# Block sums of a Strassen-like GEMM: kept in DRAM for the second layer, shared with GpSimd in the first, block maxima sought earlier

## The chip, the core and the metric

The kernel runs on one core of one Trainium2 chip. The metric is the device time of one execution in microseconds (us). A core has TensorE (PE, matmuls), VectorE (DVE), ScalarE (ACT), GpSimd (POOL) and SyncE (SP); in this kernel SP issues nearly all DMAs, in one queue and in order.

## What is computed

Two layers, the same weights in both. Sequence 2048, width 1024, 32 heads of 32, hidden width F = 3584.

```python
def _A_ref(x, wqkv, wo):                      # sliding local attention, window 8, dilation 2
    qkv = x @ wqkv ...                        # q, k, v per head
    idx = pos[:, None] - arange(8) * 2        # 8 keys per query: every second position back
    o = softmax(q . k[idx] * Dh**-0.5, masked where idx < 0) @ v[idx]
    return o @ wo
def _B_ref(x, w1, b1, w2, b2):                # MLP over the tokens
    u = gelu(einsum("bsd,sf->bdf", layernorm(x), w1) + b1)
    return transpose(einsum("bdf,fs->bds", u, w2) + b2)

x = x + _A_ref(layernorm(x)); x = x + _B_ref(layernorm(x))      # layer one
x = x + _A_ref(layernorm(x)); x = x + _B_ref(layernorm(x))      # layer two
```

## The kernel before

Each layer runs in four stages: values and attention by unit (16 units, two visits each), the output projection `out_proj` (16 row tiles, each followed by its layer norm, which writes the tile `h2[c][i]`), the first token GEMM `gemm1`, and the second, `gemm2`. TensorE is fed in a written order (`in_order`); DVE, ACT, POOL and SP operations are chained by `chain_`, which makes each come after the one before it on its engine.

**gemm1** is the stage that the change touches. F is cut into 14 blocks of 256 columns. Block 0 is done plainly (`plain`, 64 matmuls). Blocks 1 to 13 use a seven-product scheme on 2 x 2 quarters: the tokens are split by dilation class c (0, 1), the width into two halves of 512, the block's columns into two halves of 128. In fp16 that needs

- token sums T0 to T3 once in a layer (`token_sums`, `token_sums2`): T0 = B12 - B11 and T2 = B22 - B12 on POOL, T1 = B22 - T0 on DVE, T3 = B21 - T1 on POOL, eight pieces of 128x512 each;
- for every block four weight sums S0 to S3 (`weight_sum`, tile `Sw`, 128x1024 each): S0 = a01 + a11, S1 = S0 - a00, S2 = a00 - a01, S3 = a10 - S1.

Before it can be summed in fp16, a block's bf16 weights are scaled by a power of two, so that they don't leave fp16's range. The power comes from the block's largest magnitude: `top` (two DVE reductions over 128x2048, line 627), `share` (a DMA of the 128 maxima to DRAM and a DMA that broadcasts them back, lines 631 and 633), `power` (five small DVE operations, lines 638 to 643, which write the factor `cs` and its inverse `ci`). `scale_w` (line 647, ACT, two operations of 128x2048) rewrites the weights; the Gelu takes `ci` as its scale. Layer one looks for all the powers; layer two reuses them, but scales and sums the weights again.

A block fb of the loop from line 715 on, as TensorE sees it; each product is eight matmuls of 128x512, and the names P1 to P7 are used below:

| product | what | waits for, or is followed by |
|---|---|---|
| P1 | a00 x B11 into `pa` | scaled weights; then ACT copies `pa` to X (line 670) |
| P2 | a11 x T3 of the **previous** block (`product4`) | then DVE adds it to Y of that block (`py<-py,m`), ACT Gelu |
| P3 | a10 x B21, added into `pa` | then ACT Gelu of `pa` (line 674) |
| P4 | S0 x T0 into `pd` | `pa` and `pd` are halves of one PSUM tile: P4 waits for the Gelu of `pa` |
| P5, P6 | S1 x T1, S2 x T2 | ACT copies `pd` to Z after P4; DVE adds P5 to X, P6 to Y |
| P7 | S3 x B22, added into `pd` | then DVE adds `pd` to X (`px<-px,s` or `px<-px,acc`) |

Z + Y is added on POOL (`pz<-pz,py`, 128x512 in fp32). The DVE order within a block of layer one, with `nxt` = fb + 1: add `pd` to X of the previous block; `power(nxt)`; first `top` of block fb + 2; add P2 to Y of the previous block; second `top`; then S2, S0 of `nxt`, add to X, S1, add to Y, S3. The ACT order: Gelu of Z and X of the previous block, copy to X, `scale_w(nxt, 0)`, Gelu of Y of the previous block, Gelu of `pa`, `scale_w(nxt, 1)`, copy to Z.

```python
in_order(product, pa, a(fb, 1, 0), B21, False)              # P3
chain_(A, gelu, fb, 0, 0, pa)
...
in_order(product, pd, Ss[fb][:, 0], Tk(0), True, False)     # P4
```

The tiles `Sw` rotate through two buffers, which in the attention hold the zero-padded queries `qB`; the weight tiles `w` rotate through nine buffers, in which the attention's weights lie before. In the attention most of the queries are copied into `qB` by SP DMAs (line 407).

Of the kernel before, what the change touches and what calls it, by code (L numbers as in the profile page):

```python
# [10 lines left out]
ALU = mybir.AluOpType  # L11
# [17 lines left out]
def kernel(  # L29
# [38 lines left out]
    SHIFT = 14.0  # L68
    assert D == H * DH and NT == 16 and NI == 8 and NG == 8 and HG == 4
# [96 lines left out]
    ci = const.tile([P, NFB], FP32, name="ci")  # L166
    kT = [pers.tile([P, SC], BF16, name=f"kT{n}") for n in range(2)]
# [13 lines left out]
    mxd = dram.tile([NFB, P, DIL], FP32, name="mxd")  # L181

# [420 lines left out]

    def gemm1(h2, g, first):
# [7 lines left out]
        def token_sums():  # L612
            for i in range(NI):
                chain_(G, tt, nc.gpsimd, T[:, 0, i, :], B12[i], B11[i], ALU.subtract)
            for i in range(NI):
                chain_(G, tt, nc.gpsimd, T[:, 2, i, :], B22[i], B12[i], ALU.subtract)

        def token_sums2():
            for i in range(NI):
                chain_(V, tt, nc.vector, T[:, 1, i, :], B22[i], T[:, 0, i, :], ALU.subtract)  # L620
            for i in range(NI):
                chain_(G, tt, nc.gpsimd, T[:, 3, i, :], B21[i], T[:, 1, i, :], ALU.subtract)
# [12 lines left out]
        def power(fb):  # L635
            m = st("m", [P, 1])
            e = st("e", [P, 1])
            nc.vector.tensor_reduce(out=m[:], in_=bc_[fb][:], op=ALU.max, axis=AX.X)
            nc.vector.tensor_scalar(out=m[:], in0=m[:], scalar1=2.0 ** -100, scalar2=None, op0=ALU.max)
            nc.vector.tensor_scalar(out=e[:].bitcast(INT32), in0=m[:].bitcast(INT32), scalar1=0x7F800000, scalar2=None,  # L640
                                    op0=ALU.bitwise_and)
            nc.vector.tensor_scalar(out=ci[:, fb:fb + 1], in0=e[:], scalar1=2.0 ** -13, scalar2=None, op0=ALU.mult)
            return nc.vector.reciprocal(out=cs[:, fb:fb + 1], in_=ci[:, fb:fb + 1])

# [4 lines left out]
        def a(fb, c, fl):  # L649
            return w1s[fb][c][:].bitcast(FP16)[:, :, fl * P:(fl + 1) * P]  # L650

        def weight_sum(fb, n):
            if n == 2:
                Ss[fb] = qp.tile([P, 4, NI, P], FP16, name="Sw", tag="q")
            q = [Ss[fb][:, k] for k in range(4)]
            i0, i1, op = [(a(fb, 0, 1), a(fb, 1, 1), ALU.add), (q[0], a(fb, 0, 0), ALU.subtract),
                          (a(fb, 0, 0), a(fb, 0, 1), ALU.subtract), (a(fb, 1, 0), q[1], ALU.subtract)][n]
            return tt(nc.vector, q[n], i0, i1, op)
# [13 lines left out]
        def gelu(fb, fl, dc, src):  # L672
            ft = fb * GF + fl
            return nc.scalar.activation(out=g[fb][:, fl, dc * 512:(dc + 1) * 512], in_=src, func=ACT.Gelu_apprx_tanh,  # L674
                                        bias=b1_sb[:, ft:ft + 1], scale=ci[:, fb:fb + 1])

        def prepare(fb):
            if fb >= NFB:
                return
            for c in range(DIL):  # L680
                chain_(A, scale_w, fb, c)

        def finish12(fb):
            chain_(V, tt, nc.vector, X[fb][:], X[fb][:], ad[fb][:, 1, :], ALU.add)
            chain_(A, gelu, fb, 0, 1, X[fb][:])
# [5 lines left out]
        def finish21(fb):  # L691
            chain_(V, tt, nc.vector, Y[fb][:], Y[fb][:], f_[fb][:], ALU.add)
            chain_(A, gelu, fb, 1, 0, Y[fb][:])

        token_sums()
        for c in range(DIL):
            if first:
                chain_(V, top, 1, c)
        if first:
            share(1)  # L700
        token_sums2()
        plain(0, h2, g)
        load_w1(2)
        load_w1(3)
        if first:
            chain_(V, power, 1)
        prepare(1)
        if first:
            for c in range(DIL):
                chain_(V, top, 2, c)  # L710
            share(2)
        for n in (2, 0, 1, 3):
            chain_(V, weight_sum, 1, n)

        for fb in range(1, NFB):
            prev, nxt = fb - 1, fb + 1
# [3 lines left out]
            in_order(product, pa, a(fb, 0, 0), B11)  # L720
            if prev:
                finish12(prev)
            X[fb] = x2("px", [P, 512], FP32)
            chain_(A, copy, X[fb], pa)
            if first and nxt < NFB:
                chain_(V, power, nxt)
            if nxt < NFB:
                chain_(A, scale_w, nxt, 0)
            if first and fb + 2 < NFB:
                chain_(V, top, fb + 2, 0)  # L730
            if prev:
                product4(prev)
                finish21(prev)
            in_order(product, pa, a(fb, 1, 0), B21, False)
            chain_(A, gelu, fb, 0, 0, pa)
            if first and fb + 2 < NFB:
                chain_(V, top, fb + 2, 1)
                share(fb + 2)
            if fb + 3 < NFB:
                load_w1(fb + 3)  # L740
            if nxt < NFB:
                chain_(A, scale_w, nxt, 1)
                chain_(V, weight_sum, nxt, 2)
# [3 lines left out]
            if nxt < NFB:  # L747
                chain_(V, weight_sum, nxt, 0)
# [3 lines left out]
            if nxt < NFB:  # L752
                chain_(V, weight_sum, nxt, 1)
# [4 lines left out]
            chain_(G, tt, nc.gpsimd, Z[fb][:], Z[fb][:], Y[fb][:], ALU.add)  # L758
            if nxt < NFB:
                chain_(V, weight_sum, nxt, 3)  # L760
            chain_(A, gelu, fb, 1, 1, Z[fb][:])
            in_order(product, pd, Ss[fb][:, 3], B22, False)
        fb = NFB - 1
        finish12(fb)
        product4(fb)
        finish21(fb)
# [35 lines left out]
    for li in range(2):  # L802
# [24 lines left out]
        for vis in range(2 * NU):  # L827
# [9 lines left out]
            if vis == 2 * NU - 3:  # L837
                todo[:] = order
                for _ in range(3):
                    load_xr(res)  # L840
            in_order(scores, u, b)
# [4 lines left out]
            if vis:  # L846
                in_order(values, *divmod(vis - 1, 2), v, oT)
                if u + 1 < NU:
                    norm.pop()()
                else:  # L850
                    chain_("DVE", norm.pop())
            for n in range(2):
                if u + 1 < NU:
                    in_order(qk_chunk, u + 1, wts, *chunks[2 * b + n])
                    continue
                half, add, store, ln = out_proj(0, 2 * b + n, oT, wo, res, xa[li], h2)
                in_order(half, 0)
                chain_("DVE", add, 0)
                if n == 0:
                    chain_("DVE", mask, 2, 3)  # L860
                else:
                    ln_step()
                in_order(half, 1)
                chain_("DVE", add, 1)
                store()
                lns.append(list(ln))
                if n:
                    ln_step()
        in_order(values, NU - 1, 1, v, oT)
        for k, (c, i) in enumerate(order[4:]):  # L870
# [55 lines left out]
```

## Time and profile before

| | |
|---|---|
| time, median of 3 runs | 1294.91 us (1294.69 to 1295.47) |
| profiled execution | 1294.46 us, of which the span from first to last instruction is 1292.8 us |
| TensorE busy | 1248.3 us (97%) |
| VectorE, ScalarE, GpSimd busy | 647.1, 512.3, 100.8 us |
| layer one: last matmul of `plain` to P4 of block 2 | 274.46 to 312.29 us |
| layer one: P4 of block 2 to P4 of block 11 | 312.29 to 432.30 us |
| layer two: last matmul of `plain` to P1 of block 2 | 926.41 to 938.57 us |
| DMA traffic | 128.33 MB, mean 99 GB/s |

A line of the timeline reads: start in us, duration in us, engine, line of the kernel, operation, output<-inputs, shapes, count, and in brackets how long the engine had been idle and what released it. A line of the waits reads: engine and line that waited, what it waited for, then us in total, how many times, the longest. In a list by tile the three durations are the shortest, the median and the longest in ns.

### The profile page before, as it was taken

How to read it: one execution, taken by the hardware profiler on the slowest of the kernel's cores; microseconds unless marked ns; L12 is line 12 of the kernel's file. 1: busy time of each engine (PE TensorE's matmuls, PEld its weight loads, DVE VectorE, ACT ScalarE, POOL GpSimd, SP SyncE). 2: the span in 40 equal slices, each digit the busy share in tenths (PEclk: the TensorE clock that was granted, in tenths of full speed). 3: DMA queues.
4: the chain of work that ended last, by engine and by line, in shares of the span. 5: the costliest groups of instructions: out<-in, count | busy, mean ns of one | idle time of the engine just before them, and what ended most of it. 6: DMA issues, size and time to landing. Idle time of an engine off the chain costs nothing. (4 is left out here: it accounts for less than half of the span.)

```text
span 1292.8 us, 19914 instructions
## 1 busy us (share of the span) xinstructions
PE 1248.3 (97%) x8214; PEld 571.7 (44%) x8214; DVE 647.1 (50%) x1172; ACT 512.3 (40%) x751; POOL 100.8 (8%) x89
## 2 busy tenths in 40 slices
PE   9999999967999999999999999999999999999999
PEld 4444444423443444444444444444444444444444
DVE  7467777887778633232210577777843433111111
ACT  4356664444656520000023566655656564000000
POOL 0000000340010100000000000002510101000000
PEclk9999999988999999999999999999999999999999
DMA  8611124643443226545510111236522222334330
GB/s 240 111 46 49 48 83 134 197 118 67 101 78 102 66 69 172 135 128 162 145 49 1 43 50 50 80 122 196 147 79 84 69 87 66 112 106 137 116 92 33
DMA packets 207850, 128.33 MB, mean 99 GB/s; under 512 B 46352, under 2 KB 187536, under 8 KB 207760
## 3 DMA queue, kind: packets, MB, share of 16 engines
q1 hardware_dynamic: 207760, 127.07, 36.0%
q8 instruction: 64, 1.05, 0.4%
q14 instruction: 26, 0.21, 0.1%
HBM read 98.18 MB, written 16.79 MB: 89 GB/s over the span
## 5 line engine op out<-in xcount | busy, mean ns | idle before, releaser
L787 PEld LDWEIGHTS <-w 128*128 128x128 bf16 x1820 | 177.0, 98 | 210.1
L394 PE MATMUL m<-hT,wqk 128*128 128x512 bf16 x1024 | 231.7, 380 | 0.0
L787 PE MATMUL s<-g,w 128*128 128x512 bf16 (+1 forms) x924 | 202.1, 374 | 0.0
L440 DVE TENSOR_TENSOR Pm<-pc,band 32x640 bf16<-32x640 bf16 x256 | 123.6, 483 | 56.2 <-ACT pc L428 49.4
L394 PEld LDWEIGHTS <-wqk 128*128 128x128 bf16 x1024 | 95.2, 98 | 118.0 <-issue 10.7
L662 PEld LDWEIGHTS <-Sw 128*128 128x128 f16 x832 | 81.6, 98 | 132.2 <-issue 28.7
L509 PE MATMUL m<-wo,oT 128*128 128x512 bf16 x512 | 111.7, 379 | 1.2 <-DVE xn L516 1.2
L647 ACT ACTIVATE w<-w,cs 128x2048 f16<-128x2048 bf16 x52 | 103.7, 1996 | 12.6 <-DMA w<-in_B_w_dram 7.4
L195 ACT ACTIVATE ln<-mv,eps 128x1 f32<-128x1 f32 x64 | 18.8, 294 | 225.2 <-DVE mv L203 180.5
L789 DVE SCALAR_TENSOR_TENSOR xo<-s,b_sb,xs 128x512 bf16<-128x512 f32 (+1 forms) x33 | 24.4, 739 | 155.4 <-PE s L787 143.8
L787 PE MATMUL acc<-g,w 128*128 128x512 bf16 x448 | 101.1, 379 | 0.0
L662 PEld LDWEIGHTS <-w 128*128 128x128 f16 x624 | 61.3, 98 | 86.0 <-ACT w L647 9.5
L787 PE MATMUL m<-g,w 128*128 128x512 bf16 (+1 forms) x448 | 97.8, 376 | 0.0
L662 PE MATMUL m<-T,Sw 128*128 128x512 f16 x416 | 94.3, 380 | 0.0
L405 DVE COPY qB<-qs 32x512 bf16<-32x512 bf16 x136 | 38.1, 280 | 96.1 <-ACT qs L401 94.8
L662 PE MATMUL s<-h,w 128*128 128x512 bf16 x288 | 69.7, 386 | 10.4 <-ACT w L647 9.0
L509 PEld LDWEIGHTS <-oT 128*128 128x128 bf16 x512 | 49.6, 98 | 61.6 <-issue 2.8
L674 ACT ACTIVATE g<-pz,b_sb,ci 128x512 bf16<-128x512 f32 x26 | 21.1, 813 | 136.9 <-POOL pz L602 136.9
L602 POOL TENSOR_TENSOR T<-h 128x512 f16<-128x512 bf16 x16 | 18.5, 1153 | 651.8 <-DMA xr<-xb 402.6
L602 POOL TENSOR_TENSOR pz<-pz,py 128x512 f32<-128x512 f32 x26 | 39.9, 1534 | 307.4 <-DVE py L602 257.5
L627 DVE TENSOR_REDUCE mx<-w 128x1 f32<-128x2048 bf16 x26 | 59.0, 2278 | 0.0
L401 ACT CAST qs<-m 128x512 bf16<-128x512 f32 x64 | 37.5, 586 | 48.3 <-PE m L394 48.3
(105 smaller groups left out, 1379.4 us busy)
## 6 DMA issues: line engine op xcount, KB each, us to landing
w<-in_B_w_dram SPq DMA_DIRECT2D x56, 512.0 KB, 4.7
w<-in_B_w_dram SPq DMA_DIRECT2D x64, 448.0 KB, 4.4
wqk<-in_A_wqkv_dram SPq DMA_DIRECT2D x16, 512.0 KB, 5.0
xa<-xn SPq DMA_DIRECT2D x32, 256.0 KB, 2.1
xs<-xa SPq DMA_DIRECT2D x32, 256.0 KB, 3.1
wo<-in_A_wo_dram SPq DMA_DIRECT2D x8, 512.0 KB, 5.6
xr<-in_A_x_dram SPq DMA_DIRECT2D x16, 256.0 KB, 3.3
xb<-xo SPq DMA_DIRECT2D x16, 256.0 KB, 2.0
```

The costliest lines, as they stand in the source:

```text
L394: mm = nc.tensor.matmul(ps[:], lhsT=wts[part][:, kt, (g % 2) * P:(g % 2 + 1) * P], rhs=hT[:, kt, lo:lo + 512], start=(kt == 0), stop=(kt = ...
L401: nc.scalar.copy(out=qs[:], in_=ps[:])
L405: nc.vector.tensor_copy(out=qB[u % 2][hp, h, ls], in_=qs[hp, :])
L440: mm = nc.vector.tensor_tensor(out=Pm[rp, :, s0:s0 + HB, r * KG:r * KG + GW].rearrange("p h t k -> p t h k"), in0=pc[rp], in1=mk, op=ALU.mult)
L509: mm = nc.tensor.matmul(ps[:], lhsT=oT[g][:, cols(c, i)], rhs=wo[n][g // 4][:, g % 4, :], start=(g == 0), stop=(g == NG - 1))
L602: return eng.tensor_tensor(out=out, in0=a, in1=b, op=op)
L627: return nc.vector.tensor_reduce(out=bx[fb][:, c:c + 1], in_=w1s[fb][c][:], op=ALU.max, axis=AX.XY, apply_absolute_value=True)
L647: return nc.scalar.activation(out=w[:].bitcast(FP16), in_=w[:], func=ACT.Identity, scale=cs[:, fb:fb + 1])
L662: r = nc.tensor.matmul(out, lhsT=lhs[:, k, :], rhs=rhs[k], start=start and k == 0, stop=stop and k == NI - 1, skip_group_check=True)
L674: return nc.scalar.activation(out=g[fb][:, fl, dc * 512:(dc + 1) * 512], in_=src, func=ACT.Gelu_apprx_tanh, bias=b1_sb[:, ft:ft + 1], scal ...
L787: nc.tensor.matmul(ap, lhsT=w2t[ft // HF][:, ft % HF, c::DIL], rhs=g[ft // GF][:, ft % GF, lo:lo + w], start=(ft == 0), stop=(ft == FT - 1))
L789: nc.vector.scalar_tensor_tensor(out=xo[:, lo:lo + w], in0=ap, scalar=b2_sb[:, i, c:c + 1], in1=xs[:, lo:lo + w], op0=ALU.add, op1=ALU.add)
```

## The change

1. **Layer two's sums from DRAM.** In layer one each block's four sums are written to DRAM (`keep_sums`, 1 MB). Layer two loads them (`load_sums`) and neither scales nor sums: P1, P2 and P3 use the bf16 weights as they are, X is copied with the factor `cs`, and the addition of P2 to Y multiplies by `cs` (`c21`). The load of block 2's weights comes before `plain`.
2. **Z + Y on DVE** in both layers, instead of on POOL.
3. **S0 and S2 on POOL** in layer one (`sums_g`); S1 and S3 stay on DVE (`sums_v`). On DVE the order in a block becomes: add P5 to X, add P6 to Y, Z + Y, S1, S3, add `pd` to X, `power`, `top`, add P2 to Y, `top`. On ACT: copy to X, Gelu of X, Z and Y of the previous block, Gelu of `pa`, `scale_w(nxt, 1)`, copy to Z, `scale_w(nxt, 0)`. POOL takes S0 and S2 after that.
4. **T1 on POOL** in both layers: POOL does T0 as the tiles of class 0 come, then T1, T2 and T3 of each piece as the tile of class 1 comes.
5. **Maxima of blocks 1 and 2 during layer one's attention**: four extra weight loads (`pre_load`, 512 KB each), sixteen reductions of 128x512 (`pre_top`), one shared DMA round trip (`pre_share`), and `power` of both blocks in `out_proj`. Block 1's `scale_w` then stand among the layer norms of `out_proj`, as they did in layer two before.

```diff
+    def pre_load(k):
+        fb, c = divmod(k, DIL)
+        t = wt_("w1", [P, NI, FB])
+        pre[k] = t
+        return nc.sync.dma_start(out=t[:], in_=w1_v[c, :, :, (fb + 1) * FB:(fb + 2) * FB])
+    def pre_top(k, j):
+        fb, c = divmod(k, DIL)
+        return nc.vector.tensor_reduce(out=mx0[:, fb, c, j:j + 1], in_=pre[k][:, 2 * j:2 * j + 2, :], op=ALU.max, axis=AX.XY,
+                                       apply_absolute_value=True)
+    def pre_share():
+        nc.vector.tensor_reduce(out=mx1[:], in_=mx0[:].rearrange("p b c j -> p b (c j)"), op=ALU.max, axis=AX.X)
+        chain_("SP", lambda: nc.sync.dma_start(out=mxp[:], in_=mx1[:]))
+        chain_("SP", lambda: nc.sync.dma_start(out=bc0[:], in_=mxp[:].partition_broadcast(P)))
...
             for i in range(NI):
+                chain_(G, tt, nc.gpsimd, T[:, 1, i, :], B22[i], T[:, 0, i, :], ALU.subtract)
                 chain_(G, tt, nc.gpsimd, T[:, 2, i, :], B22[i], B12[i], ALU.subtract)
-        def token_sums2():
-            for i in range(NI):
-                chain_(V, tt, nc.vector, T[:, 1, i, :], B22[i], T[:, 0, i, :], ALU.subtract)
-            for i in range(NI):
                 chain_(G, tt, nc.gpsimd, T[:, 3, i, :], B21[i], T[:, 1, i, :], ALU.subtract)
...
+        def sums_g(fb):
+            sum_tile(fb)
+            chain_(G, weight_sum, nc.gpsimd, fb, 0)
+            chain_(G, weight_sum, nc.gpsimd, fb, 2)
+        def sums_v(fb):
+            chain_(V, weight_sum, nc.vector, fb, 1)
+            chain_(V, weight_sum, nc.vector, fb, 3)
+        def keep_sums(fb):
+            nc.sync.dma_start(out=sd[fb][:], in_=Ss[fb][:])
+        def load_sums(fb):
+            sum_tile(fb)
+            nc.sync.dma_start(out=Ss[fb][:], in_=sd[fb][:])
+        def copy_x(fb):
+            if first:
+                return copy(X[fb], ad[fb][:, 0, :])
+            return nc.scalar.activation(out=X[fb][:], in_=ad[fb][:, 0, :], func=ACT.Identity, scale=cs[:, fb:fb + 1])
+        def c21(fb):
+            if first:
+                return tt(nc.vector, Y[fb][:], Y[fb][:], f_[fb][:], ALU.add)
+            return nc.vector.scalar_tensor_tensor(out=Y[fb][:], in0=f_[fb][:], scalar=cs[:, fb:fb + 1], in1=Y[fb][:],
+                                                  op0=ALU.mult, op1=ALU.add)
...
         for fb in range(1, NFB):
...
             in_order(product, pa, a(fb, 0, 0), B11)
+            if first:
+                keep_sums(fb)
+            elif nxt < NFB:
+                load_sums(nxt)
+            chain_(A, copy_x, fb)
             if prev:
-                finish12(prev)
-            chain_(A, copy, X[fb], pa)
-            if nxt < NFB:
-                chain_(A, scale_w, nxt, 0)
+                add12(prev)
+                chain_(A, gelu, prev, 0, 1, X[prev][:])
+                chain_(A, gelu, prev, 1, 1, Z[prev][:])
...
             chain_(A, copy, Z[fb], pd)
-            if nxt < NFB:
-                chain_(V, weight_sum, nxt, 0)
+            if more:
+                chain_(A, scale_w, nxt, 0)
+                sums_g(nxt)
...
             chain_(V, tt, nc.vector, Y[fb][:], X[fb][:], c_[:], ALU.add)
-            chain_(G, tt, nc.gpsimd, Z[fb][:], Z[fb][:], Y[fb][:], ALU.add)
-            if nxt < NFB:
-                chain_(V, weight_sum, nxt, 3)
-            chain_(A, gelu, fb, 1, 1, Z[fb][:])
+            chain_(V, tt, nc.vector, Z[fb][:], Z[fb][:], Y[fb][:], ALU.add)
+            if more:
+                sums_v(nxt)
...
+            if first and vis % 6 == 0 and vis < 6 * DIL * NPRE:
+                chain_("SP", pre_load, vis // 6)
...
+            if first and 0 <= k < DIL * NPRE and j % 3 < 2:
+                with tc.issue_after(normed.ins):
+                    pre_top(k, j - j // 3)
+            if first and vis == 2 * NU - 4:
+                pre_share()
...
+        if first:
+            chain_("DVE", power, 1, 1 + NPRE, bc0[:].rearrange("p q b -> p b q"))
```

`more` stands for layer one with a next block, and `DIL` and `NPRE` are 2.

## The prediction, made before the changed kernel ran

> **What bounds the kernel now.** I read the engines' shares and slices first.
>
> ```profile
> PE 1248.3 (97%) x8214; PEld 571.7 (44%) x8214; DVE 647.1 (50%) x1172; ACT 512.3 (40%) x751; POOL 100.8 (8%) x89
> PE   9999999967999999999999999999999999999999
> ```
>
> TensorE does the same work before and after, so only its 44.5 us of idle time (1292.8 - 1248.3) can be gained, and a half-rate clock behind it. The waits on TensorE over the whole run say where it lies:
>
> ```profile
> PE s L662 <- ACT g L674: 19.3, 13, 7.4
> PE s L662 <- ACT w L647: 9.0, 1, 9.0
> PE acc L662 <- ACT g L674: 7.8, 8, 1.2
> ```
>
> Layer one enters `gemm1` with two long waits: 9.0 us for block 1's scaling, and 7.4 us (of the 19.3). The other 20 waits of the first and third line are P4 waiting for the Gelu of `pa`, about 1 us a block, because both halves are one PSUM tile. The change keeps that tile, so these waits stay. Third, the timeline of one block of layer one (block 2, P4 to P4):
>
> ```profile
> 312.29 1.89 PE L662 MATMUL acc<-T,Sw 128*128 128x512 f16 x8 [0.98 <-ACT g L674]
> 314.21 0.59 ACT L670 COPY pz<-acc 128x512 f32<-128x512 f32 x1
> 319.39 0.69 DVE L602 TENSOR_TENSOR px<-px,acc 128x512 f32<-128x512 f32 x1 [0.44 <-PE acc L662]
> 320.00 0.41 DVE L638 TENSOR_REDUCE m<-bc 128x1 f32<-128x256 f32 x1
> 321.08 2.28 DVE L627 TENSOR_REDUCE mx<-w 128x1 f32<-128x2048 bf16 x1
> 323.29 0.68 DVE L602 TENSOR_TENSOR py<-py,m 128x512 f32<-128x512 f32 x1
> 324.00 0.81 ACT L674 ACTIVATE g<-py,b_sb,ci 128x512 bf16<-128x512 f32 x1
> 324.72 0.76 ACT L674 ACTIVATE g<-s,b_sb,ci 128x512 bf16<-128x512 f32 x1
> 325.53 1.89 PE L662 MATMUL s<-T,Sw 128*128 128x512 f16 x8 [1.00 <-ACT g L674]
> ```
>
> The period is 13.24 us; P3 ends 0.98 before P4. From the addition of `pd` at 319.39 each line starts where the one above it ends: addition, `power`, `top`, addition of P2, Gelu of Y, Gelu of `pa`, P4. It is 6.14 us long and already without slack: **whatever delays that addition on VectorE delays the next P4**. Last, how VectorE and GpSimd stand each other:
>
> ```profile
> L602 POOL TENSOR_TENSOR T<-h x16: 1152/1153/1156, 219.0 to 894.6; 128x512 f16<-128x512 bf16 x16
> L602 DVE TENSOR_TENSOR T<-h,T x16: 411/1368/1375, 271.8 to 925.5; 128x512 f16<-128x512 bf16 x16
> 926.77 1.64 DVE L602 TENSOR_TENSOR Sw<-w 128x1024 f16<-128x1024 f16 x1
> 934.57 0.68 DVE L602 TENSOR_TENSOR Sw<-w,w 128x1024 f16<-128x1024 f16 x1
> ```
>
> GpSimd takes 1.15 us for 512 columns. A VectorE sum that takes 0.41 or 0.68 us alone takes 1.37 or 1.64 beside GpSimd (its T3 pieces run until 934.1): it waits about 0.96 of GpSimd's 1.15 us.
>
> **Layer one, the steady block.** In the changed program's order S1 and S3 stand on VectorE directly ahead of the addition of `pd`, and S1 needs S0 from GpSimd, which needs both scalings. Counted from P4: copy to Z at 1.92 (314.21 - 312.29); the next ACT operation 0.47 later (as after the copy at 308.32, followed by 308.79); the second scaling takes 1.99 and ends at 4.38; GpSimd starts 0.07 later, as after a layer norm. S0 has twice the columns of a T piece: 2 x 1.153 = 2.31, ends at 6.76. S1 and S3 alone are 2 x 0.68, with 0.1 for the signal: 8.2. Then the 6.14: P4 again at 14.35, **1.1 more than 13.24**. But S2 runs on GpSimd from 6.76 on, and one of S1 and S3 must wait for it. Scaled from the row, that wait is 0.96/1.15 of 2.31 = 1.9; no row has a piece of 1024, and it could be nothing (S1 and S3 both first) or 2.3 (all of it). I take 1.8, since the row is the same kind of operation: P4 at 16.15, **2.9 more**. Z + Y costs VectorE 0.69 but ends before S0 does, so it is paid at nothing unless it keeps S1 back (0.7); its leaving GpSimd gains nothing, because the Gelu of Z isn't what P4 waits for. Nine intervals, into P4 of blocks 3 to 11, hold the whole sequence: 9 x 2.9 = 26.1. Into block 12 there is no `top`, 2.2 less: 13.95 against 13.14, +0.8. Into block 13 neither `power` nor `top`: 0.
>
> One rule is stricter than the row. The Trainium skill, "SBUF — State Buffer", section "Who interferes with whom", says that a VectorE operation with two SBUF inputs and a GpSimd operation that reads SBUF exclude each other for the whole instruction; by it the wait would be the whole 2.31, and the nine intervals 4.6 us longer.
>
> **The clock.** A gap of 16.15 - 7 x 1.725 = 4.1 us stands before each P4. In the windows of the two long waits the granted clock falls to 0.50: the last matmul before ended at 274.46, the fall is at 277.3; and 289.67 with 294.3, so 2.8 and 4.6 us after. 4.1 lies between: I count a fall in half of the blocks. The eight matmuls after it took 3.57 us instead of 1.89 (P4 at 297.10), and P4's end starts the sequence above: 1.7 x 9 x 0.5 = 7.7 (bounds 0 and 15.3).
>
> **Layer one, the entry.** Layer two before entered without seeking maxima, with its scalings among the layer norms, so it is the pattern: last matmul of `plain` 926.41, P4 of block 1 at 931.67, 5.3 later. The scalings between the norms cost 1.2 us there (`PE m L509 <- DVE xn L516`), now here too. P4 of block 1: 274.46 + 1.2 + 5.3 = 281.0. GpSimd: 24 T pieces x 1.153 = 27.7 from the first tile of class 1 (247.3), pushed 3.1 by the scalings (5.46 instead of 2.30 us idle at 904.56): 278.1; S0 to 280.4, S2 to 282.7; S1 and S3 to 283.7. T and S are in time for P4 to P7 within half a microsecond, so T1 and T3 on GpSimd cost nothing, and 1 to 2 if the scalings come later. Then VectorE has both `top` of block 3, 4.45, to 288.2. Its maxima go round through DRAM: from issue at 285.83 to `power` at 293.07 it took 7.24, so `power` of block 3 starts at 295.5; less the first addition the sequence is 5.5: P4 of block 2 at **301.0 against 312.29, 11.3 gained**. The round trip is now last, and TensorE idles 8 us before that P4, which costs 1.7 for the clock: 9.6 net.
>
> **Layer two.** Gone: the 1.2 us wait, 0.1 of the wait for `Sw` at block 1 (the Gelu is right behind it), 0.05 a block for the scaling ahead of the Gelu (0.6). P4's 0.9 us stays. On SP the first load of sums stands before the last `qB` copy of unit 15 and waits for the scores at 848.90; the copy then goes behind 1 MB and is needed at 853.31. Behind 1 MB of `wqk` the slowest copy landed after 3.3 us against 1.9, so 0 to 1.2; I take 0.6. Every later load has a block's time. Net 1.3 gained.
>
> **The rest, at nothing.** 16 x 0.57 (a quarter of 2.28) of maxima on VectorE in the attention lie in gaps (1.45 us before the masks at 106.65); uncovered they cost 9.1. Four loads of 512 KB are queued ahead of `qB` copies as `wqk` is, which made TensorE wait 0; uncovered, 1.2 each. `pre_share` blocks SP for some 3 us, where the next copies wait for a cast 6 us later. `power` of blocks 1 and 2, 1.1 us, falls in `out_proj` where VectorE waits for products. 13 MB written and 13 read join stages at 88 and 79 GB/s; the peaks of the trace are near 350. The scalings taken off ACT in layer two free an engine that isn't the bound.
>
> **Sum**, against the profiled 1294.46 (0.45 below the median): -9.6 + 26.1 + 0.8 + 7.7 - 1.3 = +23.7, so **1318**.
>
> One more rule speaks against the change, with another price. "GPSIMD Engine Reference", section "Engine selection", has an elementwise sum on VectorE, GpSimd being about twice as slow. By that page S0 would take an estimated 1.37 (twice 0.68), against 2.31 by the row; the steady block would grow by only 1.2, no clock would fall, and the total would be about 1294. Before, 1.153 against 0.411 is 2.8 times, so I stay with the row.
>
> **Rivals.**
> - *GpSimd and VectorE don't hinder each other here.* S1 and S3 slip in before S2. For: S1 is released by S0's signal alone. Against: 1.64 in five sums in a row. P4 of block 2 at 299.0 (13.3, less 1.7); 9 x 1.1; no clock falls: -11.6 + 9.9 - 1.3 = -3.0, **1291.5**.
> - *The other side: the sums hide, the entry counts in full.* Then the period stays at 13.24, and -11.3 + 1.7 - 1.3 = -10.9 gives **1283.5**. It decides from the point where S1 and S3 end before 7.1, when the addition of `pd` can start (319.39 - 312.29); for that S0 has to take at most 1.2 us. Against: 1.153 for half the columns.
> - *The round trip is late in every block.* S0 to S3 (1 MB) and two weight loads now go ahead of the maxima; I see 2 us of margin. If it doubles, 2 us x 9 more: **1336**.
>
> **How the numbers follow.** Forecast 0.70, first rival 0.13, second 0.08, third 0.09. The forecast's own bounds: 1305 (S0 in 2.0, no clock fall) to 1330 (whole wait, every clock fall). Reaching to the first and the third rival the range is 1291 to 1336; the second and the tails stay outside. A measurement tells about 0.2%, 2.6 us, from no change: faster 0.16 (the second rival, most of the first), same 0.04, slower 0.80.
>
> **What would show it.** Right: TensorE waits of about 4 us for ACT's Gelu before P4 in layer one, periods near 16, S0 near 2.3 us on GpSimd, one of S1 and S3 well over 0.68, the granted clock at 0.5 in some blocks; no wait of 9 us at the entry. Wrong: periods at 13.2, or `pd`'s addition still right after P7.

## The result, and the profile after

The changed kernel takes 1328.66 us, the median of 4 runs (1328.20 to 1329.58), against 1294.98 for the kernel before in the same comparison: slower by 2.6%, ratio 1.0261, 95% interval 1.0243 to 1.0278. The prediction was 1318.0, with a range of 1291 to 1336. The profiled execution took 1329.58 us, its span 1327.8, which is 35.0 longer than before. (One profile among the experiments, that of late2, was taken in a disturbed execution of 1644 us and is not read; its kernel ran again as late2_again.)

The page of the kernel after, with the slices of TensorE and of its granted clock:

```profile
PE 1255.3 (95%) x8066; PEld 575.6 (43%) x8214; DVE 619.7 (47%) x1112; ACT 466.6 (35%) x725; POOL 131.8 (10%) x105
PE   9999999987777799999999999999999999999999
PEclk9999999997888999999999999999999999999999
```

VectorE and ScalarE are less busy than before, and the kernel is slower all the same. The dip in slices 9 to 14 is layer one's `gemm1`, and the clock falls there too. Before, slices 9 and 10 alone were low. The waits on TensorE over the whole run:

```profile
PE s L700 <- ACT g L718: 29.4, 15, 4.2
PE acc L700 <- ACT g L718: 22.4, 8, 7.3
PE m L515 <- DVE xn L522: 2.4, 1, 2.4
PE s L431 <- DMA qB<-qs: 1.5, 1, 1.5
```

The 9.0 us for block 1's scaling are gone, as predicted. The waits for a Gelu have grown from 27.1 to 51.8 us: P4 of blocks 3 to 11 of layer one waits 3.3 to 4.3 us each, where it was about 1. The last two lines are small waits of the prediction, both larger than it had them (1.2 and 0.6).

The timeline of the block that was shown before (block 2, P4 to P4, with lines left out):

```profile
303.00 3.57 PE L700 MATMUL acc<-T,Sw 128*128 128x512 f16 x8 [7.29 <-ACT g L718]
...
309.22 2.12 POOL L608 TENSOR_TENSOR Sw<-w,w 128x1024 f16<-128x1024 f16 x1 [16.62 <-ACT w L667]
310.89 1.01 DVE L608 TENSOR_TENSOR pz<-pz,py 128x512 f32<-128x512 f32 x1
311.31 2.57 POOL L608 TENSOR_TENSOR Sw<-w 128x1024 f16<-128x1024 f16 x1
311.82 2.61 DVE L608 TENSOR_TENSOR Sw<-Sw,w 128x1024 f16<-128x1024 f16 x1
314.46 0.69 DVE L608 TENSOR_TENSOR Sw<-w,Sw 128x1024 f16<-128x1024 f16 x1
315.07 0.68 DVE L608 TENSOR_TENSOR px<-px,acc 128x512 f32<-128x512 f32 x1
...
321.18 3.57 PE L700 MATMUL s<-T,Sw 128*128 128x512 f16 x8 [4.21 <-ACT g L718]
```

Read it from the bottom. P4 at 321.18 comes 6.11 us after the addition of `pd` at 315.07: the chain of 6.14 is unchanged. That addition starts 12.07 us after P4 instead of 7.10. Ahead of it stand S1 with 2.61 us (it runs beside S2 on GpSimd) and S3 with 0.69. S1 can't start before S0 is done, at 311.34, and stands behind Z + Y, which runs beside S0 and takes 1.01 us instead of 0.69. S0 takes 2.12 us and starts late, because P4 itself took 3.57 instead of 1.89 (behind a P4 of 1.89 us, in p1_twice below, it starts 4.60 us after P4 instead of 6.22).

In which instruction the hold falls changes from block to block. By tile, from 300 to 480 us (shortest, median and longest duration in ns), Z + Y and S1:

```profile
L608 DVE TENSOR_TENSOR pz<-pz,py x10: 871/2058/2629, 310.9 to 473.7; 128x512 f32<-128x512 f32 x10
L608 DVE TENSOR_TENSOR Sw<-Sw,w x10: 678/680/2610, 311.8 to 475.8; 128x1024 f16<-128x1024 f16 x10
```

In four of the ten blocks S1 is held (2.6 us); in the other six S2 gets in first, Z + Y is held (2.0 to 2.6) and S1 takes 0.68. S3 takes 0.69 in all ten.

### The profile page after: what moved, and what is told of

It reads as the page before. It is cut to its first block, busy times and chain, and to the rows that moved or that the text cites. A ratio compares the mean times of both kernels' runs of the same rounds, so it can differ in the third digit from the quotient of the medians.

```text
span 1327.8 us, 19719 instructions
## 1 busy us (share of the span) xinstructions
PE 1255.3 (95%) x8066; PEld 575.6 (43%) x8214; DVE 619.7 (47%) x1112; ACT 466.6 (35%) x725; POOL 131.8 (10%) x105
## 4 chain that ended last, share of the span: by engine, by line
PE 67%; DVE 6%; issue 2%; ACT 2%; DMA 0%; DVEq 0%; ACTq 0%
PE s L826 15%; PE m L700 9%; PE m L400 8%; PE m L826 7%; PE acc L826 7%; PE s L700 7%; PE m L385 4%; PE m L515 4%; PE acc L700 3%; DVE Sw L608 2%; ACT g L718 2%; DVE mx L657 1%; DVE py L608 1%; PE s L431 1%; PE acc L466 1%
## 5 line engine op out<-in xcount | busy, mean ns | idle before, releaser
L400 PE MATMUL m<-hT,wqk 128*128 128x512 bf16 x962 | 223.6, 380 | 6.2 <-issue 4.4
L700 PEld LDWEIGHTS <-Sw 128*128 128x128 f16 x832 | 85.8, 103 | 169.2 <-issue 85.4
L700 PE MATMUL m<-T,Sw 128*128 128x512 f16 x416 | 100.2, 397 | 0.0
L700 PEld LDWEIGHTS <-w 128*128 128x128 f16 (+1 forms) x624 | 60.9, 98 | 75.6 <-issue 2.0
L608 DVE TENSOR_TENSOR px<-px,m 128x512 f32<-128x512 f32 x26 | 17.9, 687 | 143.3 <-PE m L700 133.7
L700 PE MATMUL s<-T,Sw 128*128 128x512 f16 x144 | 41.8, 443 | 29.4 <-ACT g L718 29.4
L434 ACT ACTIVATE pc<-s,shift 128x640 bf16<-128x640 f32 x64 | 51.1, 799 | 13.4 <-PE s L431 13.4
L385 PE MATMUL m<-wv,hT 128*128 128x512 bf16 x251 | 55.2, 379 | 0.3
```

The source lines that it names most:

```text
L385: nc.tensor.matmul(ps[:], lhsT=hT[:, kt, cols(c, i)], rhs=wv[kt // 2][:, kt % 2, n * 512:(n + 1) * 512], start=(kt == 0), stop=(kt == KD - 1))
L400: mm = nc.tensor.matmul(ps[:], lhsT=wts[part][:, kt, (g % 2) * P:(g % 2 + 1) * P], rhs=hT[:, kt, lo:lo + 512], start=(kt == 0), stop=(kt = ...
L434: nc.scalar.activation(out=pc[:].rearrange("p (n t) h k -> p n (t h k)", n=2), in_=ss[:, :, 0:2 * HG * GW], func=ACT.Exp, scale=scale, bia ...
L608: return eng.tensor_tensor(out=out, in0=a, in1=b, op=op)
L700: r = nc.tensor.matmul(out, lhsT=lhs[:, k, :], rhs=rhs[k], start=start and k == 0, stop=stop and k == NI - 1, skip_group_check=True)
```

## The experiments

Each kernel starts from the kernel after, unless it says otherwise. The ratios are to runs of the kernel before in the same comparison (medians from 1293.6 to 1295.6). The last three columns are read from the traces: "P4(2)" is the start of P4 of block 2, "interval" the mean of the nine intervals up to P4 of block 11, "slow P4" how many of the P4 of blocks 3 to 11 took longer than 1.89 us.

| kernel | us | ratio to before, 95% | P4(2) | interval | slow P4 |
|---|---|---|---|---|---|
| before | 1294.98 | 1 | 312.29 | 13.33 | 0 |
| after | 1328.66 | 1.0261 [1.0243, 1.0278] | 303.00 | 17.98 | 9 |
| p1_twice | 1318.46 | 1.0172 [1.0157, 1.0188] | 302.47 | 16.99 | 2 |
| s2_dve | 1311.30 | 1.0117 [1.0101, 1.0132] | 302.59 | 16.02 | 6 |
| s2_halves | 1327.14 | 1.0243 [1.0230, 1.0256] | 302.37 | 17.89 | 9 |
| late_s13 | 1313.74 | 1.0133 [1.0116, 1.0150] | 305.64 | 16.40 | 6 |
| late2_again | 1305.18 | 1.0081 [1.0065, 1.0098] | 301.41 | 15.80 | 5 |
| late2_one_write | 1303.94 | 1.0079 [1.0059, 1.0098] | 301.66 | 15.91 | 4 |
| late3 | 1285.26 | 0.9940 [0.9924, 0.9955] | 300.63 | 13.64 | 0 |
| sums_back | 1279.87 | 0.9871 [0.9856, 0.9886] | 296.81 | 13.54 | 0 |
| sums_back2 | 1276.08 | 0.9847 [0.9835, 0.9860] | 293.13 | 13.51 | 0 |
| l2_alone | 1297.58 | 1.0007 [0.9997, 1.0017] | 311.05 | 13.90 | 1 |
| l2_one_write | 1291.95 | 0.9985 [0.9976, 0.9994] | 311.02 | 13.32 | 0 |

### The clock: more work in the gap

**p1_twice**

```diff
+            if first and 3 <= fb <= 11:
+                in_order(product, pa, a(fb, 0, 0), B11)
             in_order(product, pa, a(fb, 0, 0), B11)
```

> In blocks 3 to 11 of layer one P1 is computed twice into the same half (eight more matmuls, 1.73 us, the first result is overwritten): 15.5 us more work for TensorE, which shortens its idle gap before P4 from about 4 to about 2.3 us. Theory (the clock falls in that gap, and P4's slow matmuls start the next block's sequence later): P4 takes 1.89 us again in these blocks, and the kernel with more work is faster by 12 us (the measured lengthening of P4) to 15.6 us: 1313 to 1317. Rival (P4's slow matmuls are not on the path): no change, 1329. Rival (TensorE is what bounds the blocks): 1344.

Measured: 1318.46, 10.2 us faster than the kernel after (11.5 by the two ratios) with 72 more matmuls of 128x512. The timeline of TensorE:

```profile
354.54 1.89 PE L700 MATMUL acc<-T,Sw 128*128 128x512 f16 x8 [1.52 <-ACT g L718]
371.09 1.89 PE L700 MATMUL s<-T,Sw 128*128 128x512 f16 x8 [2.58 <-ACT g L718]
...
420.76 3.45 PE L700 MATMUL s<-T,Sw 128*128 128x512 f16 x8 [2.58 <-ACT g L718]
```

Behind a P4 at the full clock the block takes 16.55 us (354.54 to 371.09), with the same wait at its end, now 2.58 long. So 16.55 is what the order of the engines costs, and nearly all of the rest of 17.98 is the clock. Two of the nine P4 were still slow, one of them the last line shown, 2.0 us together; that is why the time lies 1.5 us above theory's range. Both rivals are excluded: P4's slow matmuls are on the path, and TensorE doesn't bound the blocks.

The two P4 after a wait of 2.58 us, one fast and one slow, differ in where the wait lies. In the granted clock of these traces, the falls of one trace start at multiples of 3.41 us from each other. Here one starts at 420.54, and 2.36 us of the wait before the slow P4 lie in the 3.41 us before it. The wait before the fast one is cut by that grid at 369.34, into 0.83 and 1.75 us.

### The hold: S2 taken away, or cut in two

**s2_dve**

```diff
             chain_(G, weight_sum, nc.gpsimd, fb, 0)
-            chain_(G, weight_sum, nc.gpsimd, fb, 2)
+            if fb == 1:
+                chain_(G, weight_sum, nc.gpsimd, fb, 2)
...
                 chain_(A, gelu, prev, 1, 0, Y[prev][:])
+            if first and prev:
+                chain_(V, weight_sum, nc.vector, fb, 2)
...
                 share(far)
+            if first:
+                keep_sums(fb)
```

> GpSimd keeps S0 alone; S2 goes to VectorE behind the addition of P2; S1 and S3 stay ahead of the addition of pd. Theory: the lock (S1 takes 2.60 us instead of 0.68) goes, the lateness of S0 stays. Counted from P4: second scaling ends at 4.38, S0 at 6.57, S1 and S3 at 8.0, P4 again 6.11 later, at 14.1; the gap before P4 is then 2.0 us and the clock doesn't fall. Intervals of 14.1 instead of 17.98, S1 at 0.68: about 1291. If the clock falls all the same, 1.7 us a block more: 1306. Rival (it is the lateness alone, the lock hides in it): intervals above 16, over 1312.

Since S2 now comes later, the edit also moves the write of the block's sums (`keep_sums`) behind the maxima on SyncE.

Measured: 1311.30. S1 takes 0.68 in every block: the hold is gone. From the timeline of VectorE:

```profile
326.19 0.68 DVE L608 TENSOR_TENSOR Sw<-Sw,w 128x1024 f16<-128x1024 f16 x1
...
328.91 0.42 DVE L629 TENSOR_REDUCE m<-bc 128x1 f32<-128x256 f32 x1 [0.73 <-DMA bc<-mxd]
```

But the three intervals behind a P4 at the full clock are 15.2 to 15.4, not 14.1. From P4 at 318.99 in its trace: S0 ends at 6.72 (expected 6.57); Z + Y, beside S0, takes 1.10 instead of 0.69, so that S1 starts at 7.20 and the addition of `pd` at 8.52 (expected 8.0); `power` then waits 0.73 for the maxima. The kernel after has no such wait in these blocks; it may come from the moved write, which no run separates. `power` starts 1.2 to 1.4 us after the addition in these three blocks, instead of 0.60; without that delay each of them is 14.63 us long, and 16.55 of p1_twice less 14.63 is 1.92, the hold. The gap before the next P4 is 3.2 and the clock falls in six of nine blocks. So the time lies above theory's worst case of 1306 and one us under the rival's 1312, and the mean interval of 16.02 is the rival's; its reason, that the hold hides in the lateness, is excluded by the 1.92. The mechanism is seen, the sum of small terms was too low.

**s2_halves**

```diff
-            chain_(G, weight_sum, nc.gpsimd, fb, 2)
+            for h in (slice(0, 4), slice(4, 8)):
+                chain_(G, tt, nc.gpsimd, Ss[fb][:, 2, h], a(fb, 0, 0)[:, h], a(fb, 0, 1)[:, h], ALU.subtract)
```

> The changed kernel with S2 on GpSimd cut into two instructions of 128x512 each. Theory (VectorE waits for the end of the GpSimd instruction that is under way): S1 waits for the first half only and takes about 1.6 us instead of 2.60, S3 may then wait for a part of the second half; the block is shorter by 0.5 to 1 us, the gap before P4 too, and the clock falls less often: 1310 to 1322. Rival (GpSimd keeps the memory over both, or VectorE is merely slowed in proportion): S1 still near 2.6 us, 1326 to 1331.

Measured: 1327.14, so by its time the rival holds. By tile it is the theory:

```profile
L608 POOL TENSOR_TENSOR Sw<-w x20: 1147/1599/1607, 310.6 to 473.0; 128x512 f16<-128x512 f16 x20
L608 DVE TENSOR_TENSOR Sw<-Sw,w x10: 1633/1636/1639, 311.1 to 471.9; 128x1024 f16<-128x1024 f16 x10
L608 DVE TENSOR_TENSOR Sw<-w,Sw x10: 691/1108/1528, 312.8 to 473.6; 128x1024 f16<-128x1024 f16 x10
```

S1 takes 1.64 in all ten blocks: it waits 0.96 for one half, as the row of before had it for one piece of 512. But now S3 is held by the other half by up to 0.84 us, and where S3 isn't, Z + Y is held by the first half. The engines take turns, instruction by instruction; cutting the instruction only spreads the hold.

### The place: S1 and S3 off the path

**late_s13**

```diff
                 chain_(A, gelu, prev, 1, 0, Y[prev][:])
+            late = first and prev
+            if late:
+                chain_(V, weight_sum, nc.vector, fb, 1)
...
                 chain_(V, top, far, 1)
                 share(far)
+            if late:
+                chain_(V, weight_sum, nc.vector, fb, 3)
+            if first:
+                keep_sums(fb)
...
-            if more:
-                sums_v(nxt)
```

> S1 and S3 stay on VectorE and S0 and S2 on GpSimd, but S1 goes behind the addition of P2 and S3 behind the second reduction of the maxima, so neither stands ahead of the addition of pd. Theory (place on the chain): the addition of pd is again right behind P7, the nine intervals fall from 17.98 to about 13.3 us each (-41.8), blocks 12 and 13 give back 3.05 and 2.04: about 1282 us. If S2 on GpSimd now holds up an operation of the chain for up to 1.9 us a block, up to 17 us more: 1299. Rival (GpSimd's sums, or the 13 MB written, slow VectorE wherever S1 and S3 stand): intervals stay at 16 or more, 1310 to 1329.

Measured: 1313.74, far from 1282 and in the rival's range. In the block shown the addition of `pd` is where theory puts it, but something else is late (its timeline, with SyncE's DMA issues as SPq):

```profile
323.91 0.34 SPq L661 DMA_DIRECT2D mxd<-mx  x1
324.51 0.34 SPq L692 DMA_DIRECT2D sd<-Sw  x1
329.48 0.32 SPq L663 DMA_DIRECT2D bc<-mxd  x1
333.33 0.42 DVE L629 TENSOR_REDUCE m<-bc 128x1 f32<-128x256 f32 x1 [2.82 <-DMA bc<-mxd]
```

In this block P4 starts at 322.65 and `pd` is added at 329.84, 7.19 later. Then `power` waits 2.82 for the maxima, whose way took 9.4 us (323.91 to 333.33) with the megabyte of sums issued into the middle of it. That is the prediction's third rival, made by the experiment itself: 13.24 + 2.82 is 16.1, and the gap brings the slow P4 back. In three of the nine intervals another cause shows: Z + Y, which still stands ahead of the addition of `pd`, takes 2.0 to 2.3 us beside S2, and the addition comes 10.1 to 11.0 us after P4.

**late2** writes SyncE's order out, and keeps S1 and S3 behind the second reduction:

```diff
+            if first and prev:
+                chain_("Q", keep_sums, prev)
...
-                share(far)
+                chain_("Q", share, far)
+            if first and prev:
+                sums_v(fb)
             if fb + 3 < NFB:
-                load_w1(fb + 3)
+                chain_("Q", load_w1, fb + 3) if first else load_w1(fb + 3)
...
-            if more:
-                sums_v(nxt)
```

> S1 and S3 stay on VectorE and S0 and S2 on GpSimd, but both S1 and S3 go behind the second reduction of the maxima. SyncE's order in layer one's blocks is written out: maxima out, maxima back, next weights, and only then the sums of the block before to DRAM, so that the megabyte written is not ahead of the maxima, as it was in late_s13, where it was issued 0.6 us behind them and the power waited up to 2.8 us for them. Theory (place on the chain): the addition of pd at 7.1 to 7.2 us after P4 and no wait for the maxima: intervals of 13.3 instead of 17.98, blocks 12 and 13 as before the change: 1279 to 1287 us. Rival (in late_s13 it was not the megabyte: GpSimd's sums and the traffic are too much anyhow): 1305 or more.

Measured: 1301.08, 1306.05 and 1308.83 (ratio 1.0074, 1.0051 to 1.0097), far above theory, two of them in the rival's range. Two more runs looked for what is left.

> late2 once more, for its blocks: its time of 1301 to 1309 us is 20 above what the place on the chain alone gives. If the maxima are what holds it (they share the queues with a megabyte of sums and two loads of weights in each block): intervals of about 15 us, the addition of pd at 7.2 us after P4, and 1 to 2.5 us of VectorE waiting for the maxima before the power. If VectorE itself is too full, or held by GpSimd: no such wait, and operations of the chain longer than alone. 1301 to 1309 us.

> late2, with the sums of block 1 alone written to DRAM; layer two loads block 1's sums for every block, so that its results are left out of account, with the same instructions and bytes loaded. 12 MB less written in layer one. If the megabyte per block holds up the maxima: intervals of 13.3 to 13.6 us and no wait for the maxima, 1280 to 1288 us. If it is something else (GpSimd's sums, VectorE's load): as late2, 1301 to 1309.

late2_again took 1305.18, and late2_one_write 1303.94, within its spread: 12 MB less written changes nothing here, and the theory of the megabyte fell for this kernel. The trace of late2_again shows three causes, which take turns. First, in the block from 317.53 Z + Y on VectorE takes 2.41 us, because S2 has started first, and it stands ahead of the addition of `pd`. Second, in the next block `power` waits 1.25 for the maxima. Third, the reduction behind it waits 1.59 for a load of weights, which the written order had put behind the maxima. The gaps make P4 slow in five blocks of nine. late2_one_write shows the same three.

**late3** is late2 with the first and the third taken away: Z + Y on GpSimd behind S2, and the next weights ahead of the maxima.

```diff
+            if first and fb + 3 < NFB:
+                chain_("Q", load_w1, fb + 3)
             if seek:
                 chain_(V, top, far, 1)
-                share(far)
+                chain_("Q", share, far)
...
-            chain_(V, tt, nc.vector, Z[fb][:], Z[fb][:], Y[fb][:], ALU.add)
+            if first:
+                chain_(G, tt, nc.gpsimd, Z[fb][:], Z[fb][:], Y[fb][:], ALU.add)
+            else:
+                chain_(V, tt, nc.vector, Z[fb][:], Z[fb][:], Y[fb][:], ALU.add)
```

> late2 with two more edits in layer one: Z + Y goes back to GpSimd, behind S2, so that no addition that GpSimd can hold up stands ahead of the addition of pd; and SyncE's order is sums of the block before, next weights, maxima out, maxima back. Theory (late2 kept 15 to 16 us a block because Z + Y on VectorE was held by S2 for up to 2.28 us instead of 0.69, a load of weights 0.75 behind its use, and waits for the maxima of up to 1.3): the addition of pd at 7.1 to 7.2 us after P4 in every block, intervals of 13.3 to 13.9, few slow P4: 1281 to 1289 us. Rival (the round trip of the maxima is what is left, with GpSimd's 5.9 us a block or without): intervals above 14.5, 1296 to 1306.

Measured: 1285.26, faster than before by 0.6%, with S0 and S2 on GpSimd as in the change. Its timeline, from P4 to P4:

```profile
329.89 1.89 PE L700 MATMUL s<-T,Sw 128*128 128x512 f16 x8 [1.40 <-ACT g L718]
...
336.57 2.12 POOL L608 TENSOR_TENSOR Sw<-w 128x1024 f16<-128x1024 f16 x1
337.06 0.69 DVE L608 TENSOR_TENSOR px<-px,s 128x512 f32<-128x512 f32 x1 [1.09 <-PE s L700]
...
343.17 1.89 PE L700 MATMUL acc<-T,Sw 128*128 128x512 f16 x8 [1.03 <-ACT g L718]
```

`pd` is added 7.17 us after P4, beside S2 and at 0.69 as if alone; the interval is 13.28 and no P4 of blocks 3 to 11 is slow. So S0 at 2.12 us on GpSimd costs the block nothing in this place (13.28 against 13.24 before). What cost was that VectorE's path to P4 ran through operations that wait for GpSimd's result or are held by it. late3 also differs from the kernel after in SyncE's order, but that can't be the cause there: in the kernel after VectorE waits neither for maxima nor for weights in these blocks.

### The rest of the change

**sums_back**: layer one's blocks in the order of before, all four sums on VectorE and Z + Y on GpSimd there; everything else of the change stays.

```diff
-            sums_g(1)
-            sums_v(1)
+            sum_tile(1)
+            for n in (2, 0, 1, 3):
+                chain_(V, weight_sum, nc.vector, 1, n)
...
```

> Layer one's blocks as before the change (all four sums and their places on VectorE, Z + Y on GpSimd, the old order on ScalarE), and the rest of the change: maxima of blocks 1 and 2 in the attention, T1 on GpSimd, layer two's sums from DRAM. Theory (all the loss lies in the order of layer one's blocks, the other parts gain): intervals of 13.3, entry 9.3 us earlier with 1.7 lost to the clock, about 2.6 gained in layer two: 1294.98 - 7.6 - 2.6 = 1284.8 us (1281 to 1288). Rival (the writes of the sums or the maxima cost too): no faster than 1292.

Measured: 1279.87, 5 us better than theory and just under its range. The entry is the reason: P4 of block 2 at 296.81 instead of 303.00, with no slow P4. The blocks give 1.9 us back (13.54 against 13.33, by waits for the maxima), and layer two gained 1.1, not 2.6. First the kernel after, then sums_back (timeline):

```profile
280.46 2.60 DVE L608 TENSOR_TENSOR Sw<-Sw,w 128x1024 f16<-128x1024 f16 x1 [9.08 <-POOL Sw L608]
283.69 4.47 DVE L657 TENSOR_REDUCE mx<-w 128x1 f32<-128x2048 bf16 x2
297.48 0.42 DVE L629 TENSOR_REDUCE m<-bc 128x1 f32<-128x256 f32 x1 [3.00 <-DMA bc<-mxd]
```

```profile
276.87 4.46 DVE L657 TENSOR_REDUCE mx<-w 128x1 f32<-128x2048 bf16 x2
```

In the kernel after VectorE sits idle for 9.08 us until GpSimd has done S0 of block 1, with the reductions for block 3 queued behind S1. In sums_back they start 6.8 us earlier, `power` at 291.30 finds the maxima there, and their way through DRAM is no longer last.

**sums_back2** moves three things more: block 1's scalings behind the last layer norm, the reductions for block 3 ahead of block 1's sums, the first load of sums in layer two behind the last layer norm.

```diff
+            last[A] = last["NORM"]
             for c in (1, 0):
                 chain_(A, scale_w, 1, c)
...
```

`last[A] = last["NORM"]` puts what follows on ScalarE behind the last layer norm.

> sums_back with three places moved: block 1's scalings in layer one behind the last layer norm; the reductions for block 3 ahead of block 1's sums on VectorE; the first load of sums in layer two behind the last layer norm. Theory: the wait in the output projection (2.3 us) and the slow matmuls behind it (24 in 6.98 us, 1.7 more than at the full clock) go, and the 1.4 us before the last scores of layer two: 1279.9 - 5.4 = 1274.5 us (1273 to 1277). Rival (block 1's scalings and sums are then too late for its products, or the maxima of block 3 come 2 to 3 us late): 1278 or more.

Measured: 1276.08, the fastest of all, 1.5% under before. P4 of block 1 came at 279.90 instead of 283.59: the 2.3 us wait in `out_proj` and the slow matmuls behind it are gone. The third move missed: the wait of 1.5 us for the last `qB` copy is still there, so its cause isn't settled.

**l2_alone** and **l2_one_write**: the kernel before with layer two's part (T1 on GpSimd, too), and the same with one write.

```diff
-            nc.sync.dma_start(out=Ss[fb][:], in_=sd[fb][:])
+            nc.sync.dma_start(out=Ss[fb][:], in_=sd[1][:])
...
-            if first:
+            if first and fb == 1:
                 keep_sums(fb)
```

> The kernel before with layer two's sums from DRAM alone (written in layer one, loaded in layer two, no scaling and summing there, Z + Y of layer two on VectorE, T1 on GpSimd); layer one's entry and blocks as before. The prediction counted 1.3 us gained: 1293.6. The changed kernel lost 37.6 us up to P4 of block 13 and 33.4 to 35 in all, which would be 2.6 to 4 gained: 1291 to 1292.5. Rival (the 13 MB written and read back cost what the sums cost): 1295 or more.

> l2_alone, with the sums of block 1 alone written in layer one and loaded for every block of layer two (the results of layer two left out of account, its instructions and bytes the same). l2_alone's trace has intervals of layer one that are 5.1 us longer in all than before, with 0.3 to 1.7 us of waiting for the maxima in five blocks. If the 12 MB written cause these: 1291 to 1293.5 us (layer two's gain of 2.6 to 3.0 us from its output projection on, less 0.9 more for the last copy of the queries). If not: 1295 to 1298 as l2_alone.

l2_alone took 1297.58, ratio 1.0007 with 1 inside the interval: no gain, and both expected gains missed. Its twelve executions spread from 1294.0 to 1299.2 us, four of them under 1295, and the trace is of one at 1297.7. l2_one_write took 1291.95, as expected if the writes are the cause; by its ratio that is 0.15% or 1.9 us gained, and the two intervals don't overlap. The blocks of the two traces say where (13.90 against 13.32 us). The maxima of the block where the wait was longest (SyncE and `power`), l2_alone first:

```profile
352.98 0.34 SPq L658 DMA_DIRECT2D mxd<-mx  x1
361.83 0.42 DVE L626 TENSOR_REDUCE m<-bc 128x1 f32<-128x256 f32 x1 [1.72 <-DMA bc<-mxd]
```

```profile
351.99 0.34 SPq L658 DMA_DIRECT2D mxd<-mx  x1
359.04 0.41 DVE L626 TENSOR_REDUCE m<-bc 128x1 f32<-128x256 f32 x1
```

From issue to `power` the maxima take 8.9 us instead of 7.1; the broadcast back is issued 4.4 us after the way out (at 357.41) instead of 3.0 (354.99). Most blocks differ less: from issue to the landing of the broadcast the median is 7.2 us against 6.9. Where blocks take 13.3 us a late one costs time; in the kernel after, with 18 us a block, the same way took 8.5 us in the median, and yet no `power` of blocks 4 to 11 waited: the writes were hidden by the loss.

## Why the prediction was right, point by point

The time lay in the range, near the top of the forecast's own bounds (1305 to 1330), and the mechanism is the predicted one: the sums on VectorE ahead of the addition of `pd`, late because of S0, held by S2, with the 6.14 us chain behind them. late3 takes S1, S3 and Z + Y off that path, leaves S0 and S2 on GpSimd, and the loss is gone. The size was not right: the loss is 34 us where 23.7 were forecast, and all five terms erred to the same side. The sum, term by term (us of the span):

| term | predicted | measured | from |
|---|---|---|---|
| P4 of block 2, before any slow P4 counts | -11.3 | -9.3 | 303.00 - 312.29 |
| nine intervals at the full clock | +26.1 | +29.0 | 9 x (16.55 - 13.33), 16.55 of p1_twice |
| slow P4, blocks 2 to 11 | +9.4 (1.7 + 7.7) | +13.8 | their durations, less 10 x 1.89 |
| blocks 12 and 13, besides | +0.8 | +1.9 | 16.19 - 13.14 - 1.68; 16.07 - 14.03; less 1.5 for seven matmuls of `gemm2` that now run ahead of P4 of block 13 (16 instead of 9) |
| layer two and the rest | -1.3 | -1.1 | P4 of block 13 to the end: 830.7 against 833.3, plus the same 1.5 |
| sum | +23.7 | +34.3 | the span grew by 35.0 |

- **The block.** At the full clock it is 16.55, where 16.15 was forecast: 1.4 for lateness (14.63 - 13.24) instead of 1.1, and 1.92 for the hold instead of 1.8. S0 was 2.12, not 2.31, so the doubled row of 512 columns was 0.2 too high. The term that failed is Z + Y, "paid at nothing unless it keeps S1 back (0.7)": it does, by 0.4 to 0.5, since it stands beside S0 and takes 1.10. And in six blocks of ten it is the operation that S2 holds, in place of S1 (by 1.3 to 1.9 us).
- **The clock.** The mis-sized term: "a fall in half of the blocks". It fell in all nine (P4 took 2.53 to 3.57), at waits of 3.3 to 4.3 us, and cost 12.1 us where 7.7 were counted. The two falls of the profile before, 2.8 and 4.6 us after the last matmul, were taken as bounds of one threshold. They are not: the clock falls on a grid of 3.41 us, so the distance from the last matmul says where the gap lay on that grid, and not how long a gap has to be (last section).
- **Blocks 12 and 13.** Block 12 was priced without the hold (+1.4 measured). Into block 13 the prediction had 0: S1 is held there too, and the clearing of `qB` (1.78 us on VectorE, at 491.18) now stands between S1 and S3. Three quarters of the 2.0 us that this costs TensorE fills with matmuls of `gemm2`.
- **The entry.** P4 of block 1 came at 283.5, not 281.0: the scalings between the norms cost a wait of 2.4 instead of 1.2, and the matmuls behind it ran at the half clock. In sums_back2 P4 of block 1 comes 3.7 us earlier, and P4 of block 2 with it. In the kernel after, the late P4 of block 1 didn't delay P4 of block 2: VectorE's reductions for block 3 start at 283.69, as forecast (283.7). That the maxima's way would be last at P4 of block 2 was right (wait 7.29, predicted 8). The term that was mis-sized is this way: 9.29 us from issue (288.19) to `power` (297.48), where 7.24 was taken from the profile before, and that is the missing 2.0 us. A megabyte of sums was issued 4.35 us ahead of it; that this is the cause isn't shown.
- **Layer two.** The gain in its `gemm1` was larger than counted (1.4 from P4 of block 1 to P4 of block 13, counted 0.6), and the `qB` copy cost 1.5, above its bound of 1.2. The 2.6 us that sums_back and l2_alone were expected to gain held the 1.5 us of `gemm2`, which are no gain. "13 MB written ... at nothing" holds in blocks 4 to 11 of the kernel after and fails where the blocks are short (l2_alone against l2_one_write: 9 x 0.58 = 5.2 us by the two traces, 2.8 by the ratios).
- **The rivals.** No hindrance (1291.5): excluded by S1 at 2.61 and Z + Y at 2.63. The sums hide (1283.5): not in this order; late3 with 1285 is that case, made by moving them off the path. The maxima late in every block (1336): not in the kernel after, where they are late once, at the entry, but it appeared in late_s13 as soon as the blocks got shorter.

Of the two rules that were weighed for the hold, the row came nearer in size (1.8 for 1.92, against the whole of S2), and the runs agree with the strict one on how it works. In the block shown S1 starts 0.51 us after S2 and ends 0.55 after S2's end, so that all but 0.13 of its 0.68 us lies behind S2. The Trainium skill, "SBUF — State Buffer", section "Who interferes with whom", calls the contention for the shared ports an exclusive lock and has the issue order decide who waits. The exchange between Z + Y and S1 agrees, and so does s2_halves, where S1 waits for one half alone (0.96 us). The section also lets a VectorE operation with one SBUF input pass; in late3 the addition of `pd`, whose other input is the PSUM tile, took 0.69 beside S2.

On the price of a sum, "GPSIMD Engine Reference", section "Engine selection", has about twice VectorE's; measured are 2.12 against 0.68, 3.1 times.

## What to carry to other kernels

Before an operation is given to a slower, idle engine, follow the queue of the engine that reads its result: what stands behind the reader inherits the delay. If the reader can wait, put it behind the path, and with it every operation that the slower engine can hold up; here that, with SyncE's order written out, turned a loss of 2.6% into a gain of 0.6%, with the four sums on the same engines as in the change. When a long stage is shortened, look again at the transfers that it had covered.

## What the runs showed of the hardware

- **The clock's edge.** Over blocks 3 to 11 of all the traces in the table: after a wait of up to 2.17 us before P4 no P4 was slow; after 2.19 to 2.58 us 11 of 22 were; from 2.79 us on 31 of 31. The granted clock in these traces explains the mixed middle: in each trace the stretches of half clock up to 1250 us last 3.41, 6.83 or 10.24 us and start on one grid of 3.41 us. Counted by the windows of this grid from 20 to 1250 us, in the twelve traces that have such a stretch, each of the 61 full-rate windows in which TensorE was idle for 2.02 us or more was followed by half clock, and none of the 4175 with 1.90 us or less. So a gap counts by what of it falls into one window, and the 31 of 31 may hold only for where these gaps lay. The Trainium skill, "TensorE: Matmul & The Clock Gate", section "What's actually happening", puts the fall after at least one idle window of about 3.4 us, with windows that run freely. The traces agree on the window; they differ in that it need not be idle as a whole, since 2.02 us of 3.41 were enough.
- **A busier TensorE can be faster.** 72 useless matmuls in the gaps saved 10.2 us here, because they kept seven of nine P4 at the full clock.
- **Turns.** VectorE and GpSimd alternate instruction by instruction on the operations with two SBUF inputs seen here: S1 took 2.61 instead of 0.68 beside S2, and S2 itself took 2.57 instead of 2.12 when Z + Y had got in first.
